# Two blocks' squares and scalings moved head by head to ScalarE, and one batch's last k and v loaded earlier

## The chip, the cores and the metric

The kernel runs on one NeuronCore of a Trainium2 chip. The metric is the device time of one execution in microseconds. The engines are TensorE (PE; PEld is its weight load), VectorE (DVE), ScalarE (ACT), GpSimd (POOL) and SyncE (SP, which here only issues transfers). Each takes its instructions in the order of its own queue and waits for semaphores of the others.

## What is computed

The reference chains three layers over 8 batches of 576 tokens, with 8 heads of 64 columns (4608 tokens, 512 columns):

```python
kv = np.einsum('bhsd,bhse->bhde', k, v)
out = np.einsum('bhsd,bhde->bhse', q, kv)
rms = np.sqrt(np.mean(out * out, axis=-1, keepdims=True) + 1e-06)
x = (out / rms * g_norm)                    # tokens x 512
h = x @ w_in                                # 512 x 2048
x = (np.maximum(h, 0) + alpha * np.minimum(h, 0)) @ w_out
logits = x @ w_gate; e = argmax(logits)     # one of 8 experts for each token
out[token] = gate_w * sigmoid(x @ w_output_gate)[e] * (relu(x @ w1[e]) @ w2[e])
```

The norm is one of each head: 64 columns are squared and summed for each token and head, and the head is multiplied by one number. This is where the change sits.

## The kernel before

Tokens are handled in 12 blocks of 384, three tiles of 128 tokens each. Products with weights are done in fp16 halves (a high and a low half for each f32 number), so x and every weight are split into halves first; the tiles of x are turned by a DMA before they serve as operand of the first dense layer.

The first two blocks are emitted by hand. The string `plan` is a list of words, and each word emits a few instructions; under `tc.manual_schedule` the queues of PE, DVE, ACT and SP keep exactly this order. Only POOL's order, and all that comes after the plan, is set by a scheduler. The plan mixes three things: the attention of blocks 0 and 1 (tiles 0 to 5), reading and splitting the 32 pieces of w_in and w_out, and the dense layers of blocks 0 and 1 as far as weights are ready.

The words for a tile t of attention: `q`/`Q` turn q by PE and copy it (ACT); `p` multiplies by kv into a PSUM bank (`ops`); `P` is `squares`: ACT writes the squares of the bank to `xs`; `s` is `sums`: DVE adds each head's 64 squares (`st`), scales them (`ms`), and POOL raises them to the power -1/2 (`rs`); `e` takes, once for each block, the exponents that put rows in fp16's range (DVE, small); `x` is `scaled`: DVE multiplies `rs` by the exponent and the bank by `rs`, head by head, into `xs`; `X`, `z`, `Z` make the high half (ACT), the low half (DVE) and issue the DMA that turns both (SP). A bank is free for other work of PE once `x` has read it. For block 0, `s`, `e` and `x` need all three tiles; tile 3 follows in the same queues.

The words for a weight piece i: `L` loads it (SP) into one of five raw buffers (`rawp`), `A` takes absolute values (ACT), `M` their maximum (DVE), `B` converts the bits (DVE, three instructions), `S` and `T` make the halves. A raw buffer is free after `B`, for the last four pieces of w_out after `T`. `H`, `C`, `R`, `G` are products, copy, leaky ReLU and halves of the first dense layer, `Y` the second.

k and v of a batch come as four pairs of heads; `n` is `load_kv`: two transfers (k, v) of a pair into a pool `kvp` with two buffers each, and with the first pair also the remainder of 64 rows (`kr`, `vr`). `k` is `kv_step`: PE multiplies a pair. In the plan pairs are loaded by `n` words. For batch 2 and later, which is handled after the plan, a step itself issues the load of the pair two further on, so pairs 2 and 3 of batch 2 are loaded once steps 0 and 1 are done. The first weights of the experts (`rawe`) use the five raw buffers next.

Of the kernel before, what the change touches and what calls it, by code (L numbers as in the profile page):

```python
# [10 lines left out]
F32 = mybir.dt.float32  # L11
F16 = mybir.dt.float16
BF16 = mybir.dt.bfloat16
I32 = mybir.dt.int32
AF = mybir.ActivationFunctionType
ALU = mybir.AluOpType
AX = mybir.AxisListType
# [3 lines left out]
P = 128  # L21
B, H, S, D = 8, 8, 576, 64
# [9 lines left out]
NPAIR = H // 2  # L32
TB = 3
# [3 lines left out]
QJ = 4  # L37
# [29 lines left out]
def body(ctx: ExitStack, tc, q, k, v, g_norm, w_in, w_out, alpha, w_gate, w_og, w1, w2, out):  # L67
    nc = tc.nc
    pe, dve, act, pool, sp = nc.tensor, nc.vector, nc.scalar, nc.gpsimd, nc.sync
# [36 lines left out]
    for G in range(B // 2):  # L106
        for half in range(2):
            b = 2 * G + half
# [52 lines left out]
    small = ctx.enter_context(tc.tile_pool(name="small", bufs=3))  # L161
# [27 lines left out]
    def right(name, bufs):  # L189
        return AR.enter_context(tc.tile_pool(name=name, bufs=bufs, side="right"))  # L190
# [4 lines left out]
    rawp, stg, cv = right("rawp", 5), right("stg", 2), right("cv", 2)  # L195
    kvp, qp, at = right("kvp", 2), right("qp", 2), right("at", 2)
# [16 lines left out]
    def load_kv(n):  # L213
        if n < len(kv_order):
            b, hp = kv_order[n]
            for nm, src in (("k", k), ("v", v)):
                if hp == 0:
                    t = kvp.tile([SR, H, D], F32, tag=nm + "r", name=f"{nm}r_{b}", bufs=1)
                    sp.dma_start(out=t, in_=src[b, :, QJ * P:S, :].rearrange("h p d -> p h d"))
                    kv_in[nm + "r", b] = t  # L220
                t = kvp.tile([P, 2, QJ, D], F32, tag=nm, name=f"{nm}_{b}_{hp}")
                sp.dma_start(out=t, in_=src[b, 2 * hp:2 * hp + 2, 0:QJ * P, :]
                             .rearrange("h (p j) d -> p h j d", j=QJ))
                kv_in[nm, n] = t
# [27 lines left out]
    def kv_step(n, pool_=None, tag="a"):  # L252
        b, hp = kv_order[n]
        kk, vv = kv_in.pop(("k", n)), kv_in.pop(("v", n))
        kr, vr = kv_in["kr", b], kv_in["vr", b]

        if hp % 2 == 0:
            kv_ps[b, hp // 2] = (pool_ or ps_a).tile([P, 2, D], F32, tag=tag, name=f"kvps_{b}_{hp}")
        ps = kv_ps[b, hp // 2]
        with tc.issue_after(paced["pe"]) if b > 2 else nullcontext():  # L260
            for j in range(QJ + 1):
                for i in range(2):
                    x, y = (kr[:, 2 * hp + i, :], vr[:, 2 * hp + i, :]) if j == 0 else (kk[:, i, j - 1, :], vv[:, i, j - 1, :])
                    pe.matmul(ps[64 * i:64 * i + 64, hp % 2, :], x, y, start=(j == 0), stop=(j == QJ))
        if b > 1:
            if hp % 2 == 1:
                kv_copy(n)
            load_kv(n + 2)

    def kv_copy(n):  # L270
        b, hp = kv_order[n]
        for i in range(2):
            sl = slice(64 * i, 64 * i + 64)
            (act.copy if b < 2 else dve.tensor_copy)(out=kvbd[b % 2][sl, hp - 1:hp + 1, sl], in_=kv_ps[b, hp // 2][sl])
# [19 lines left out]
    def att_parts(i):  # L294
        G, t0 = divmod(i * TB, 9)
# [3 lines left out]
        tiles = {}  # L299
# [59 lines left out]
        def squares(t):  # L359
            ops = tiles[t]  # L360
            xs = at.tile([P, DM], F32, tag="xs", name=f"xs_{G}_{t}", bufs=3)
            act.activation(out=xs, in_=ops.rearrange("p a b -> p (a b)"), func=AF.Square)
            tiles[t] = ops, xs

        def sums(t):
            nm = f"_{G}_{t}"
            ops, xs = tiles[t]
            if "st" not in tiles:
                tiles["st"] = small.tile([P, TB, H], F32, tag="st", name=f"st_{i}")
                tiles["qm"] = small.tile([P, TB], F32, tag="qm", name=f"qm_{i}")  # L370
            st = tiles["st"][:, t - t0, :]
            dve.tensor_reduce(out=st, in_=xs.rearrange("p (h d) -> p h d", h=H), axis=AX.X, op=ALU.add)
            if split_q:
                for _ in range(2):
                    dve.tensor_tensor(out=st, in0=st, in1=qi_[t], op=ALU.mult)
            ms = small.tile([P, H], F32, tag="ms", name="ms" + nm)
            dve.tensor_scalar(out=ms, in0=st, scalar1=1.0 / D, scalar2=EPS, op0=ALU.mult, op1=ALU.add)
            rs = small.tile([P, H], F32, tag="rs", name="rs" + nm)
            pool.tensor_tensor(out=rs, in0=ms, in1=mhalf, op=ALU.pow)  # L379
            tiles[t] = ops, xs, rs  # L380
# [15 lines left out]
        def scaled(t):  # L396
            ops, xs, rs = tiles[t]
            qm = tiles["qm"][:, t - t0:t - t0 + 1]
            if split_q:
                dve.scalar_tensor_tensor(out=rs, in0=rs, scalar=qm, in1=qi_[t], op0=ALU.mult, op1=ALU.mult)  # L400
            else:
                dve.tensor_scalar(out=rs, in0=rs, scalar1=qm, scalar2=None, op0=ALU.mult)
            dve.tensor_tensor(out=xs.rearrange("p (h d) -> p h d", h=H),  # L403
                              in0=ops.rearrange("p a (h d) -> p (a h) d", h=2),
                              in1=rs.unsqueeze(2).to_broadcast([P, H, D]), op=ALU.mult)

        def high(t):
            nm = f"_{G}_{t}"
# [12 lines left out]
        def x_turned(t):  # L421
            x16 = tiles.pop(t)[1]
            if i not in xt:
                xt[i] = xp.tile([P, 2 * NC, BLK], F16, tag="x", name=f"x_{i}")
            sp.dma_start_transpose(out=xt[i][:, :, (t - t0) * P:(t - t0 + 1) * P],
                                   in_=x16.rearrange("p a b -> p (a b)"))

        return ts, dict(q=turned, Q=turned_copy, t=tr, p=products, P=squares, s=sums, e=exponents, x=scaled, X=high, z=low,
                        Z=x_turned)

    def att_steps(i):
# [13 lines left out]
        if i == 2:  # L445
            for hp in range(NPAIR):
                kv_step(4 * nxt + hp)
                yield
            kv_halves(nxt)
            return  # L450
        kvs = [] if nxt is None or nxt >= B else [partial(kv_step, 4 * nxt + hp) for hp in range(NPAIR)]
        if kvs:
            kvs.append(partial(kv_halves, nxt))
# [947 lines left out]
    def emit(word):  # L1401
# [7 lines left out]
        elif what == "F":  # L1409
            y_scaled(*map(int, rest))  # L1410
        elif what in "UuVvW":
            scales(what, rest[0], int(rest[1]))
        elif rest[:1] in ("i", "o"):
            weights(what, dense[rest[0]], int(rest[1], 16))
        elif what == "k":
            n = int(rest)
            kv_step(n, *((ps_a, "a") if n < NPAIR else (ps_y, "y")))
        elif what == "c":
            scale_all()
        elif what in "fnNK":  # L1420
            dict(f=load_kv_first, n=load_kv, N=load_q, K=kv_copy)[what](int(rest))
        elif what == "D":
            i, u = map(int, rest)
            act.copy(out=accs[i][:, u, :], in_=ybank[i, u])
        elif what == "t":
            u = int(rest[1])
            src = accs[0][:, u, :]
            if rest[0] == "a":
                held["t", u] = row_scale(0, u, src, states[0][1])
            else:  # L1430
                (row_high, row_low)["bc".index(rest[0])](u, src, held["t", u])
        elif what == "q":
            t = int(rest)
            parts[t]["q"](t, *((ps_h, "h") if t < TB else (ps_y, "y") if t < 2 * TB else (ps_a, "a")))
        elif what == "e":
            parts[3 * int(rest)]["e"](3 * int(rest), 3 * int(rest) + 2)
        else:
            parts[int(rest)][what](int(rest))
# [15 lines left out]
    R021 Aie Lod Wo2 Loe H020 G021 n8 C022 Aif R022 H023 So9 Mie Soa n9 To9 F021 Bie F121 Y012 C023 G022 Sob  # L1454
    R023 Lof Aoc Mif F020 Y112 Bif F022 C020 So8 Tob G023 Aod H120 To8 F122 Ui3 Moc Mod ui3 H123 Bod C120 Vi3
    Y110 R020 Toa C123 Boc G020 vi3 F120 H121 R123 Aoe Wi3 Aof Moe G123 Y021 Sie Boe Sif Sid Sic Tie Y022 Tid
    Tif Tic R120 Mof H030 C121 Uo3 G120 Bof H130 C030 R121 R030 G121 G030 H032 C130 R130 uo3 G130 H033 Vo3 C032
    R032 G032 vo3 C033 H031 Wo3 Y121 c C031 Sof Sod Soc R031 Y020 F032 Tof G031 Toc F131 F031 Tod Soe R033 H132
    F030 Toe G033 H133 C132 R132 G132 Y031 C133 R133 G133 Y032 D01 ta1 Y030 D02 tb1 ta2 Y120 tc1 D00 tb2 ta0 q6
    tc2 F130 tb0 q7 Q6 tc0 q8 Q7 p6 H131 Q8 P6 s6 p7 C131 R131 p8 P7 G131 s7 Y122 P8 s8 e2 x6 Y130 F132 x7 X6 z6  # L1460
# [110 lines left out]
```

## Time and profile before

| | |
|---|---|
| median of three runs | 1340.95 us (1336.63 to 1350.32) |
| profiled execution | 1344.24 us |
| its span, first to last instruction | 1342.5 us |
| PE busy, share of the span | 1267.3 us, 94% |
| DVE busy | 824.4 us, 61% |
| ACT busy | 558.0 us, 42% |
| POOL busy | 413.7 us, 31% |
| mean granted clock of PE | 0.985 |

An engine is busy while an instruction of its own executes; waits and issues are not counted. The share is a mean over stages: in the page's 40 slices of 33.6 us, DVE is at nine tenths or more in the second to fourth and PE at five to eight in the first four; later PE is mostly at nine and DVE falls. The granted clock is TensorE's, as a share of full speed. A releaser (`<-`) is the instruction whose semaphore ended an engine's idle time.

### The profile page before, as it was taken

The numbers are of one execution on the slowest core, as the hardware profiler recorded it, in microseconds if no ns is written. First come the engines' busy times: TensorE is split into PE (matmuls) and PEld (weight loads), VectorE is DVE, ScalarE is ACT, GpSimd is POOL, SyncE is SP. The second block draws the span as 40 slices with busy tenths as digits, with TensorE's granted clock in tenths as the row PEclk, the third lists the DMA queues.
The fourth block names the chain that finished last, engine by engine and source line by source line (L and its number), as shares of the span: only waits on it lengthen the run. The fifth ranks groups of instructions, "written<-read, shape, count | busy, mean of one in ns | idle before, by whom it ended". The sixth has DMA issues, their size and how long they took to land. (4 is left out here: it accounts for less than half of the span.)

```text
span 1342.5 us, 22080 instructions
## 1 busy us (share of the span) xinstructions
PE 1267.3 (94%) x7681; PEld 661.5 (49%) x7681; DVE 824.4 (61%) x2254; ACT 558.0 (42%) x928; POOL 413.7 (31%) x490
## 2 busy tenths in 40 slices
PE   5688998999999989999999999999999999999998
PEld 4444455545454545545555555454434444444443
DVE  7999866989697877668687877463622221221221
ACT  4455553646564554555555665350111111111111
POOL 4322221544343442324242433222322222222211
PEclk9899998999999999999999999999999999999999
DMA  9563217695866756497745665209999799799842
GB/s 307 157 170 117 68 63 183 154 243 122 252 189 217 208 129 168 129 242 198 197 119 168 153 187 125 93 14 316 193 285 203 145 299 280 157 223 247 162 103 55
DMA packets 322497, 236.22 MB, mean 176 GB/s; under 512 B 245436, under 2 KB 278220, under 8 KB 317904
## 3 DMA queue, kind: packets, MB, share of 16 engines
q1 hardware_dynamic: 303760, 189.05, 56.3%
q0 software_dynamic: 9216, 28.94, 6.8%
q10 hardware_dynamic: 9408, 16.79, 3.7%
q8 instruction: 62, 1.02, 0.3%
q14 instruction: 51, 0.42, 0.1%
HBM read 252.54 MB, written 53.25 MB: 228 GB/s over the span
## 5 line engine op out<-in xcount | busy, mean ns | idle before, releaser
L766 PE MATMUL y<-wo,g 128*128 128x512 f16 x1728 | 394.2, 382 | 9.0 <-DVE xs L403 5.8
L726 PE MATMUL h<-x,wi 128*128 128x384 f16 x1920 | 336.8, 329 | 16.6 <-ACT m L732 15.8
L726 PEld LDWEIGHTS <-wi 128*128 128x128 f16 x2304 | 222.6, 99 | 176.5 <-issue 31.9
L766 PEld LDWEIGHTS <-g 128*128 128x128 f16 x1728 | 166.7, 98 | 202.2 <-issue 13.0
L749 POOL TENSOR_TENSOR g<-r,g 128x384 f16<-128x384 f32 x112 | 117.6, 1052 | 294.4 <-ACT g L748 235.8
L1276 DVE CAST h_d<-br_d 128x512 f16<-128x512 f32 x62 | 26.7, 430 | 257.2 <-DMA hT_d<-h_d 122.9
L742 DVE SCALAR_TENSOR_TENSOR r<-m,alphat 128x384 f32<-128x384 f32 x192 | 133.2, 696 | 31.0 <-ACT m L732 27.5
L748 ACT CAST g<-r 128x384 f16<-128x384 f32 x192 | 97.2, 509 | 116.6 <-DVE r L742 116.1
L1292 PEld LDWEIGHTS <-hT_d 128*128 128x128 f16 x744 | 72.8, 98 | 93.1 <-DMA hT_d<-h_d 4.1
L1270 PEld LDWEIGHTS <-byT_d 128*128 128x128 f16 x744 | 72.6, 98 | 88.2 <-issue 0.8
L732 ACT ACTIVATE m<-h,scal 128x384 f32<-128x384 f32 x160 | 92.1, 577 | 53.0 <-PE h L726 51.2
L379 POOL TENSOR_TENSOR rs<-ms,mhalf 128x8 f32<-128x8 f32 x36 | 66.2, 1839 | 135.1 <-DVE qm L385 87.0
L479 DVE SCALAR_TENSOR_TENSOR wlo_w<-rawe,es_w,whi_w 128x1024 f16<-128x1024 f32 x64 | 84.4, 1324 | 28.0 <-ACT whi_w L478 13.3
L1296 POOL DMA_INDIRECT out_dram<-ob_d,oidx_d x31 | 32.5, 1050 | 195.6 <-ACT ob_d L1295 185.2
L1274 ACT ACTIVATE br_d<-bh_d 128x512 f32<-128x512 f32 x62 | 37.0, 597 | 127.4 <-PE bh_d L1270 113.0
L1292 PE MATMUL bo_d<-lane,hT_d 128*128 128x512 f16 x360 | 81.7, 384 | 3.0 <-DMA hT_d<-h_d 3.0
L478 ACT ACTIVATE whi_w<-rawe,es_w 128x1024 f16<-128x1024 f32 x64 | 72.2, 1142 | 29.3 <-DMA ws<-whi_w 14.2
L1270 PE MATMUL bh_d<-lane,byT_d 128*128 128x512 f16 x360 | 80.2, 379 | 0.0
L1295 ACT ACTIVATE ob_d<-bo_d,msc_d 128x512 f32<-128x512 f32 x31 | 21.3, 687 | 141.0 <-PE bo_d L1292 141.0
L628 ACT ACTIVATE eab_w<-rawe 128x1024 bf16<-128x1024 f32 x64 | 66.6, 1051 | 25.6 <-DMA rawe<-in_moe_w_dram 21.8
L726 PE MATMUL hbank<-x,wi 128*128 128x384 f16 x384 | 67.0, 332 | 6.7 <-DMA x<-x 4.9
L913 POOL DMA_INDIRECT ytab<-row,pos x36 | 42.1, 1168 | 73.4 <-DMA ytab<-row,pos 42.6
(386 smaller groups left out, 1594.2 us busy)
## 6 DMA issues: line engine op xcount, KB each, us to landing
lane<-ws SPq DMA_DIRECT2D x74, 1024.0 KB
wi<-ws SPq DMA_DIRECT2D x44, 1024.0 KB
wo<-ws SPq DMA_DIRECT2D x36, 1024.0 KB
rawe<-in_moe_w_dram SPq DMA_DIRECT2D x64, 512.0 KB
ws<-whi_w ACTq DMA_DIRECT2D x64, 256.0 KB
ws<-wlo_w SPq DMA_DIRECT2D x64, 256.0 KB
rawwi<-in_moe_w_in_dram SPq DMA_DIRECT2D x16, 512.0 KB
rawwo<-in_moe_w_out_dram SPq DMA_DIRECT2D x16, 512.0 KB
```

Source lines behind the costliest of these rows:

```text
L379: pool.tensor_tensor(out=rs, in0=ms, in1=mhalf, op=ALU.pow)
L478: act.activation(out=dst_h, in_=src, func=AF.Copy, scale=s)
L479: dve.scalar_tensor_tensor(out=dst_l, in0=src, scalar=s, in1=dst_h, op0=ALU.mult, op1=ALU.subtract)
L628: act.activation(out=ab.rearrange("p a b -> p (a b)"), in_=raws[4 * m + i], func=AF.Abs)
L726: t = pe.matmul(ps, wi[:, f // 4 * NC + c, w, fs], xt[i][:, xc, :], start=(n == 0), stop=(n == 3 * NC - 1))
L732: t = act.activation(out=r0, in_=ps, func=AF.Copy, scale=(scst if start else scal)[:, f:f + 1])
L742: t = dve.scalar_tensor_tensor(out=r, in0=r0, scalar=alphat[:, f:f + 1], in1=r0, op0=ALU.mult, op1=ALU.max)
L748: act.copy(out=hi, in_=r)
L749: (pool if start or f % 2 else dve).tensor_tensor(out=lo, in0=r, in1=hi, op=ALU.subtract)
L766: t = pe.matmul(ps, g[:, t, f % GF, us], wo[:, f, w, :], start=(start and m == 0), stop=(stop and m == 2), **kw)
L1270: pe.matmul(hp[ts], j["yT"][:, x, ts], w1_[:, w, c, hs], start=(m == 0), stop=(m == 3 * NC - 1))
L1292: pe.matmul(po[ts], hT[:, g, ts], w2_[:, w, f, :], start=(m == 0), stop=(m == 3 * NFE - 1))
```

## The change

Three things are edited. In blocks 0 and 1 (`i < 2`), `squares` becomes eight activations of 64 columns, each with an accumulator output that gives the head's sum, so that DVE's sum goes; and `scaled` becomes eight ACT copies of 64 columns, each with the head's `rs` as scale, in place of DVE's multiplication. Block 2 and later keep the old form. Pairs 2 and 3 of batch 2 (n = 10 and 11) are loaded by two new words of the plan, `n10 n11`, behind the bits of w_out's last piece, into raw buffers instead of `kvp`. And the steps of batch 2 no longer load two pairs further on; its last step loads the first two pairs of batch 3.

```diff
@@ load_kv
-                t = kvp.tile([P, 2, QJ, D], F32, tag=nm, name=f"{nm}_{b}_{hp}")
+                if n in (4 * 2 + 2, 4 * 2 + 3):
+                    if nm == "k":
+                        both = rawp.tile([P, 512, 2], I32, tag="raw", name=f"kv_{b}_{hp}")
+                        both = both.rearrange("p a b -> p (a b)").bitcast(F32).rearrange(
+                            "p (x h j d) -> p x h j d", x=2, h=2, j=QJ)
+                    t = both[:, "kv".index(nm)]
+                else:
+                    t = kvp.tile([P, 2, QJ, D], F32, tag=nm, name=f"{nm}_{b}_{hp}")
@@ kv_step
-            load_kv(n + 2)
+            for m in ((n + 2,) if b > 2 else (n + 1, n + 2) if hp == NPAIR - 1 else ()):
+                load_kv(m)
@@ squares
-            act.activation(out=xs, in_=ops.rearrange("p a b -> p (a b)"), func=AF.Square)
+            if i < 2:
+                src = ops.rearrange("p a (h d) -> p (a h) d", h=2)
+                for h in range(H):
+                    act.activation(out=xs[:, h * D:(h + 1) * D], in_=src[:, h, :], func=AF.Square,
+                                   accum_out=tiles["st"][:, t - t0, h:h + 1])
+            else:
+                act.activation(out=xs, in_=ops.rearrange("p a b -> p (a b)"), func=AF.Square)
@@ sums
-            dve.tensor_reduce(out=st, in_=xs.rearrange("p (h d) -> p h d", h=H), axis=AX.X, op=ALU.add)
+            if i >= 2:
+                dve.tensor_reduce(out=st, in_=xs.rearrange("p (h d) -> p h d", h=H), axis=AX.X, op=ALU.add)
@@ scaled
-            dve.tensor_tensor(out=xs.rearrange("p (h d) -> p h d", h=H),
-                              in0=ops.rearrange("p a (h d) -> p (a h) d", h=2),
-                              in1=rs.unsqueeze(2).to_broadcast([P, H, D]), op=ALU.mult)
+            src = ops.rearrange("p a (h d) -> p (a h) d", h=2)
+            if i < 2:
+                for h in range(H):
+                    act.activation(out=xs[:, h * D:(h + 1) * D], in_=src[:, h, :], func=AF.Copy, scale=rs[:, h:h + 1])
+            else:
+                dve.tensor_tensor(out=xs.rearrange("p (h d) -> p h d", h=H), in0=src,
+                                  in1=rs.unsqueeze(2).to_broadcast([P, H, D]), op=ALU.mult)
@@ plan
-    Tif Tic R120 Mof H030 C121 Uo3 G120 Bof H130 C030 R121 R030 G121 G030 H032 C130 R130 uo3 G130 H033 Vo3 C032
+    Tif Tic R120 Mof H030 C121 Uo3 G120 Bof n10 n11 H130 C030 R121 R030 G121 G030 H032 C130 R130 uo3 G130 H033 Vo3 C032
```

The queue of ACT in block 0, from the third tile's squares to the fourth's (the last number of a name's first three is the tile; `kvbd` belongs to k and v, `uwo` to the weights). Before:

```order
L362 ACTIVATE xs_0_2_509<-ops_0_2_480 128x512
L517 ACTIVATE uwo3_531<-rawwo3_420 128x512
L274 COPY kvbd1_206<-kvps_1_0_495 64x2x64 x2
L414 CAST x16_0_0_556<-xs_0_0_447 128x512
L414 CAST x16_0_1_560<-xs_0_1_478 128x512
L414 CAST x16_0_2_563<-xs_0_2_509 128x512
L362 ACTIVATE xs_0_3_566<-ops_0_3_551 128x512
```

Now:

```order
L376 ACTIVATE xs_0_2_521,st_0_448<-ops_0_2_493 128x64 x8
L536 ACTIVATE uwo3_549<-rawwo3_420 128x512
L282 COPY kvbd1_206<-kvps_1_0_507 64x2x64 x2
L421 ACTIVATE xs_0_0_447<-ops_0_0_424,rs_0_0_471 128x64 x8
L421 ACTIVATE xs_0_1_484<-ops_0_1_458,rs_0_1_505 128x64 x8
L433 CAST x16_0_0_588<-xs_0_0_447 128x512
L421 ACTIVATE xs_0_2_521<-ops_0_2_493,rs_0_2_547 128x64 x8
L433 CAST x16_0_1_599<-xs_0_1_484 128x512
L433 CAST x16_0_2_602<-xs_0_2_521 128x512
L376 ACTIVATE xs_0_3_605,st_1_606<-ops_0_3_583 128x64 x8
```

Three rows became forty, and the scalings, which stood in DVE's queue, now stand between the third tile's squares and the fourth's.

The queue of SP after the plan's last weight load (`yT` are turned rows of block 0's result, `k_3_0` is pair 0 of batch 3). Before:

```order
L616 DMA rawe_0_2287<-in_moe2_w1_dram 128x1024
L616 DMA rawe_1_2289<-in_moe2_w1_dram 128x1024
L616 DMA rawe_2_2291<-in_moe2_w1_dram 128x1024
L616 DMA rawe_3_2293<-in_moe2_w1_dram 128x1024
L616 DMA rawe_4_2295<-in_moe2_w2_dram 128x2x512
L425 DMA_TRANSPOSE x_2_2109<-x16_0_6_2090 128x8x128
L425 DMA_TRANSPOSE x_2_2109<-x16_0_7_2093 128x8x128
L425 DMA_TRANSPOSE x_2_2109<-x16_0_8_2113 128x8x128
L833 DMA_TRANSPOSE yT_0_0_2141<-row0_193 128x8x128
L833 DMA_TRANSPOSE yT_0_1_2143<-row1_194 128x8x128
L232 DMA q_1_0_2147<-in_q_dram 128x8x128
L232 DMA q_1_2_2149<-in_q_dram 128x8x128
```

Four transfers of k and v of pairs 2 and 3 (`k_2_2`, `v_2_2`, `k_2_3`, `v_2_3`) came next. Now, from the new loads on, and then what stands behind q:

```order
L229 DMA kv_2_2_1774<-in_k_dram 128x2x256
L229 DMA kv_2_2_1774<-in_v_dram 128x2x256
L229 DMA kv_2_3_1777<-in_k_dram 128x2x256
L229 DMA kv_2_3_1777<-in_v_dram 128x2x256
L635 DMA rawe_0_2363<-in_moe2_w1_dram 128x1024
L635 DMA rawe_1_2365<-in_moe2_w1_dram 128x1024
L635 DMA rawe_2_2367<-in_moe2_w1_dram 128x1024
```

```order
L239 DMA q_1_2_2231<-in_q_dram 128x8x128
L229 DMA k_3_0_2283<-in_k_dram 128x2x256
L219 DMA kr_3_2281<-in_k_dram 64x8x64
L219 DMA vr_3_2285<-in_v_dram 64x8x64
L229 DMA v_3_0_2287<-in_v_dram 128x2x256
L229 DMA k_3_1_2289<-in_k_dram 128x2x256
L229 DMA v_3_1_2291<-in_v_dram 128x2x256
L635 DMA rawe_3_2369<-in_moe2_w1_dram 128x1024
L635 DMA rawe_4_2371<-in_moe2_w2_dram 128x2x512
```

The loads of batch 2's last pairs moved ahead of the expert weights, batch 3's first loads took their place behind q, and two expert loads moved behind those.

PE's queue after the plan (steps of k and v of batch 2, then h of block 2). Before, where pairs 2 and 3 followed only after 43 matmuls of h:

```order
L264 MATMUL kvps_2_0_2151<-v_2_1_1483,k_2_1_1481 64x64 x8
L264 MATMUL kvps_2_2_2182<-vr_2_1456,kr_2_1452 64x64 x2
L726 LDWEIGHTS wi_203
L726 MATMUL h_2_0_2237<-x_2_2109,wi_203 128x384
```

Now:

```order
L271 MATMUL kvps_2_0_2235<-v_2_1_1561,k_2_1_1559 64x64 x8
L271 MATMUL kvps_2_2_2258<-vr_2_1534,kr_2_1530 64x64 x2
L271 MATMUL kvps_2_2_2258<-kv_2_2_1774 64x64 x8
L271 MATMUL kvps_2_2_2258<-vr_2_1534,kr_2_1530 64x64 x2
L271 MATMUL kvps_2_2_2258<-kv_2_3_1777 64x64 x8
L745 LDWEIGHTS wi_203
L745 MATMUL h_2_0_2313<-x_2_2193,wi_203 128x384
```

All four steps now stand together, and batch 3's first step follows 36 matmuls of h and eight of the gate's logits later.

## Rows read from the trace of the kernel before

**Rows 1.** Stretches: length; PE, PEld, DVE, ACT, POOL busy; PE clock, DMA share, GB/s.

```profile
27.50:31.77 4.27, 4.27 (x52) 3.69 (x52) 4.17 (x8) 3.85 (x8) 2.55 (x2) 1.00 1.04 403
50.00:80.00 30.00, 21.81 (x95) 10.45 (x96) 28.61 (x72) 13.29 (x23) 7.73 (x6) 0.83 0.44 116
80.00:135.00 55.00, 49.83 (x280) 26.79 (x279) 52.56 (x117) 31.51 (x59) 16.61 (x14) 1.00 0.45 139
135.00:200.00 65.00, 63.17 (x379) 34.18 (x378) 49.15 (x120) 37.22 (x68) 18.81 (x17) 1.00 0.21 66
214.00:225.00 11.00, 8.54 (x70) 4.92 (x68) 5.27 (x12) 2.43 (x4) 0.73 (x1) 0.69 0.93 250
```

**Rows 2.** Waits of DVE from 11 to 80 us: total, times, longest.

```profile
DVE wi L559 <- ACT wi L557: 0.5, 1, 0.5
DVE r L742 <- ACT m L732: 0.3, 1, 0.3
```

**Rows 3.** PE in order of time: start, duration, instructions [idle before, releaser].

```profile
50.27 7.04 PE L726 MATMUL hbank<-x,wi 128*128 128x384 f16 x32 [2.83 <-DMA x<-x]
...
65.76 7.94 PE L766 MATMUL y<-wo,g 128*128 128x512 f16 x24 [5.85 <-DVE xs L403]
...
78.78 11.86 PE L726 MATMUL hbank<-x,wi 128*128 128x384 f16 x72 [2.07 <-DMA x<-x]
```

**Rows 4.** DVE in order of time, blocks 0 and 1.

```profile
32.51 0.08 DVE L524 DVE_READ_ACCUMULATOR uwo<-uwo 128x1 f32 x1
32.51 0.68 DVE L372 TENSOR_REDUCE st<-xs 128x8 f32<-128x512 f32 x1
33.23 0.18 DVE L377 TENSOR_SCALAR ms<-st 128x8 f32<-128x8 f32 x1
...
34.77 0.69 DVE L403 TENSOR_TENSOR xs<-ops,rs 128x512 f32<-128x512 f32 x1
...
39.76 0.17 DVE L377 TENSOR_SCALAR ms<-st 128x8 f32<-128x8 f32 x1
...
64.92 0.69 DVE L403 TENSOR_TENSOR xs<-ops,rs 128x512 f32<-128x512 f32 x1
...
68.22 0.69 DVE L419 TENSOR_TENSOR x<-xs,x 128x512 f16<-128x512 f32 x1
```

**Rows 5.** ACT's groups by form: shapes, count, busy us, mean ns, idle before.

```profile
L362 ACT ACTIVATE xs<-ops 128x512 f32<-128x512 f32 x36 | 21.3, 591 | 10.3 <-PE ops L353 9.8 <-PE ops L356 0.5
...
L274 ACT COPY kvbd<-kvps 64x128 f32<-64x128 f32 x8 | 2.0, 255 | 0.7 <-PE kvps L264 0.6
...
L478 ACT ACTIVATE wg<-wgr,swg 128x16 f16<-128x16 f32 x4 | 0.9, 300 | 0.0
```

**Rows 6.** ACT in order of time: squares of tiles 0, 2 and 3.

```profile
27.50 0.60 ACT L362 ACTIVATE xs<-ops 128x512 f32<-128x512 f32 x1 [0.18 <-PE ops L356]
...
31.77 0.58 ACT L362 ACTIVATE xs<-ops 128x512 f32<-128x512 f32 x1
...
38.06 0.60 ACT L362 ACTIVATE xs<-ops 128x512 f32<-128x512 f32 x1
```

**Rows 7.** PE in order of time, after the plan.

```profile
207.81 6.01 PE L726 MATMUL h<-x,wi 128*128 128x384 f16 x36 [0.54 <-DMA x<-x]
...
216.99 0.69 PE L264 MATMUL kvps<-v,k 128*64 128x64 f32 x16 [1.82 <-DMA v<-in_v_dram]
...
218.57 1.12 PE L264 MATMUL kvps<-v,k 128*64 128x64 f32 x16 [0.64 <-DMA v<-in_v_dram]
...
221.47 3.67 PE L726 MATMUL h<-x,wi 128*128 128x384 f16 x12
```

**Rows 8.** SP's queue in order of time: issue, duration, transfers.

```profile
171.43 3.55 SPq L616 DMA_DIRECT2D rawe<-in_moe_w_dram  x4
...
210.33 1.50 SPq L222 DMA_DIRECT2D k<-in_k_dram  x1
211.88 0.46 SPq L222 DMA_DIRECT2D v<-in_v_dram  x1
```

More of the change, by code (lines that the diff above doesn't have):

```diff
@@ L361, in squares @@
             xs = at.tile([P, DM], F32, tag="xs", name=f"xs_{G}_{t}", bufs=3)
-            act.activation(out=xs, in_=ops.rearrange("p a b -> p (a b)"), func=AF.Square)
+            if "st" not in tiles:
+                tiles["st"] = small.tile([P, TB, H], F32, tag="st", name=f"st_{i}")
+                tiles["qm"] = small.tile([P, TB], F32, tag="qm", name=f"qm_{i}")
+            if i < 2:
[5 more added lines that the diff above has]
+                act.activation(out=xs, in_=ops.rearrange("p a b -> p (a b)"), func=AF.Square)
             tiles[t] = ops, xs
@@ L367, in sums @@
             ops, xs = tiles[t]
-            if "st" not in tiles:
-                tiles["st"] = small.tile([P, TB, H], F32, tag="st", name=f"st_{i}")
-                tiles["qm"] = small.tile([P, TB], F32, tag="qm", name=f"qm_{i}")
             st = tiles["st"][:, t - t0, :]
-            dve.tensor_reduce(out=st, in_=xs.rearrange("p (h d) -> p h d", h=H), axis=AX.X, op=ALU.add)
+            if i >= 2:
+                dve.tensor_reduce(out=st, in_=xs.rearrange("p (h d) -> p h d", h=H), axis=AX.X, op=ALU.add)
             if split_q:
```

## The prediction, made before the change was run

> **What bounds the kernel now.** I began with the run's totals: the profiled execution took 1344.24 us, its span is 1342.5 us, and TensorE (PE) is busy in 94% of it. The chain of waits of the page does not help here: it begins only after 1121 us, and everything that is edited runs before about 220 us. So I cut that part into stretches [rows 1]. From 135 to 200 us PE is busy in 63.17 of 65 us: there it is the bound, and nothing that it is late by can be made up. From 50 to 135 us VectorE (DVE) is busy in 81.2 of 85 us, PE in 71.6: there DVE sets the pace. The waits of DVE confirm it: between 11 and 80 us it has waited 0.8 us for others, all told [rows 2]. PE's own rows in this part show what it waits for [rows 3]: for the x tiles of block 0 at 50.27 us, for a PSUM bank that DVE's scaling frees at 65.76 us (5.85 us), and for the x tiles of block 1 at 78.78 us. All three end the same path: squares, sums, exponents, scaling, fp16 halves, a turning DMA. A change of that path's length moves PE by as much, and since the later stretches are full, it stays to the end.
>
> **The change on DVE.** Six sums over 128x512 and six scalings of 128x512 go. A sum lasts 0.68 us and a scaling 0.69; the next instruction starts 0.72 after a sum, of which some 0.1 is a wait for its result [rows 4], so one holds the queue for about 0.60. That is 12 x 0.6 = 7.3 us less work on the engine that sets the pace. It would be the gain, if DVE never had to wait for what replaces it.
>
> **The change on ScalarE (ACT).** Each of six tiles gets 8 squares of 128x64 with an accumulator output, and 8 copies of 128x64 with a scale read from a column, in place of one square of 128x512 and of DVE's scaling. Neither form is in the trace, so I bound both. From PSUM, 512 columns take 591 ns and 128 take 255 [rows 5]: 0.875 ns a column, so 64 columns take 255 - 56 = 199 ns. Neighbours can overlap: the four 128x16 with a column scale take 300 ns each and 0.9 us in all, so they start 0.20 us apart, 0.10 less than they last [rows 5]. The accumulator has to be read out; DVE's own reading shows as a row of 0.08 us, and the next instruction starts at the same time as it [rows 4].
> - A head's square: at least 0.10 us (overlapped, the reading free), at most 0.40 (no overlap, and the reading as dear as a whole small instruction, 0.20). I take 0.30 = 199 ns + 0.1 for the reading, without overlap, because a reading must follow the end of what it reads. A tile's squares: S = 2.4 us (0.8 to 3.2).
> - A head's scaled copy: 0.20 us apart at 16 columns, and 48 columns more by 0.875 ns: 0.24 us; at most 0.34, without overlap. A tile: C = 1.9 us (1.6 to 2.7).
>
> **Block 0, along ACT's queue.** ACT's order is written out, so nothing overtakes. The first square starts at 27.50 and the third at 31.77 [rows 6]. Between them ACT was busy for 3.85 us [rows 1], two squares of some 0.55 and 2.75 us of other work. Now: 27.50 + 3 x 2.4 + 2.75 = 37.45 for the end of the third tile's squares. From the sum's follower on DVE (33.23) to the first scaling (34.77) it is 1.54 us [rows 4], unchanged, since the exponents stay on DVE: the first scaling starts at 39.1, 4.3 us later than before. Then three scalings and three casts stand in ACT's queue ahead of the fourth tile's squares: 3 x 1.9 + 3 x 0.52 = 7.3 us (a cast taken as the 591 ns of 512 columns less some overlap), so those start at 46.4 instead of 38.06 [rows 6], and end at 48.8. DVE takes that tile's statistics before the bits of w_out's pieces 2 and 3. It did so at 39.76 [rows 4], and now does at 48.8: **9.05 us late**, with some 13 us of DVE idle in which its saving of four sums and three scalings disappears. What is queued behind it: those bits free the raw buffer that SP's next load of w_out waits for, and behind that load stands the last turning DMA of block 0. So PE's start at 50.27 moves by the same 9 us, and DVE's weights too.
>
> **Block 1.** Here two more sums leave a DVE that has no gap: 9.05 - 1.2 = 7.85. The first scaling goes from 64.92 [rows 4] to 72.8, PE's bank is free at 74.7 instead of 65.6, three scalings end at 78.5 (3 x 1.9), and one cast later the first low half starts on DVE at 79.0, where it was 68.22 [rows 4]. That is **+10.7 us** at the x tiles for which PE waits at 78.78 [rows 3]. From there to 200 us DVE and PE have the same work as before and both are that much later, so the 10.7 us stay.
>
> By the Trainium skill, ScalarE: Activation LUTs, section What ACT_TABLE_LOAD costs, an ACTIVATE takes 186 ns plus 0.833 ns a column, a pointer operand adds 93 ns, and neighbours overlap by 93 ns. That would make a head's square 0.146 us without its reading, which the page does not price, and a copy 0.239; by the same steps the delay would be 6.0 us, and the time 1343.5. For 128 columns it gives 293 ns where the row shows 255 [rows 5]. The same page's Rules for kernel authors put multiplications on VectorE, not ScalarE; in this trace one f32 tile of 128x512 from PSUM is no dearer on ACT (0.59) than on DVE (0.69) [rows 5, 4], so what speaks against the change here is eight starts in place of one, not the engine.
>
> **The early transfers.** Before, PE stopped at 216.99 (1.82 us) and 218.57 (0.64) for batch 2's k and v, whose loads were issued only at 210.33 and behind [rows 7, 8], and the stretch 214 to 225 ran at a granted clock of 0.69 [rows 1]: 12 matmuls took 3.67 us in it, where 36 take 6.01 elsewhere [rows 7]. Idle and clock together cost 5.1 us there; 0.54 us of waiting for x at 207.81 would be covered too. Those four transfers now stand where the first expert weights were issued, at 171.43 [rows 8], 35 us before they are used, in a stretch with a DMA share of 0.21 [rows 1]: they are there in time. But the same place of SP's queue is now taken by batch 3's loads, six of them, behind the same two turning DMAs. The first v landed 216.99 - 211.88 = 5.1 us after its issue [rows 8, 7]; the remainder of batch 3's v is third in the line, so it lands near 217. PE now reaches it after the two k-v steps that it no longer skips (1.4 us from 207.27, where it began to wait for x), 36 matmuls of h (6.01) and eight small ones (0.2): 214.9 [rows 7]. About 2 us of the wait stay, with a part of the clock. Gain 3.5 us, between 1 (the wait only changes its name) and 6 (it goes whole). Two expert loads now come after batch 3's. They are the last two of five and are used in turn, so the first three cover them, and I cost that at nothing; if they were late, ACT's absolute values of expert weights would be, which PE needs only at the end of the kernel.
>
> **Sum.** 10.7 - 3.5 = +7.2 us against the profiled 1344.24: 1351.4. The median of the runs is 1340.95, 3.3 below the profiled one, so I predict **1348 us**.
>
> **Rivals.**
> 1. ACT's pieces are cheap (S = 0.8, C = 1.6). Same steps: statistics 1.8 us late, first low half of block 1 2.65 late; with a transition gain of 5 us that is 1338.6. For it: ACT is idle for half of the part, and 0.20 us apart is measured. Against: a reading per head. 20%.
> 2. ACT's pieces are dear (S = 3.2, C = 2.7), and the wait at the third tile's squares decides: statistics 14.7 late, block 1's low half 18.9 late, the transition gives 2: 1357.8, slower by over 1%. The point is about 0.36 us per head for squares with 0.28 for copies. Against: it needs no overlap anywhere. 17%.
> 3. DVE's relief reaches the end: ACT is never waited for, 7.3 + 5.6 us are won: 1328. For it: DVE has no gap. Against: the third scaling and the fourth square are one after another in one queue. 5%.
> 4. The transfers are not early: the second waits in SP's queue until w_out's piece 12 is split and its buffer free. The expert loads of before waited for the same buffers and were out by 175 us [rows 8], so I give it 3%; it would be 1351.
>
> My forecast has 55%: between +2 and +13 us.
>
> **Numbers.** 1% (13.4 us) is about what a measurement here can tell from no change. The range takes the forecast, the cheap case and most of the dear one: 1337 to 1361. Faster by over 1%: 6% (rival 3 and a little). Slower: 22% (rival 2 and the upper end of the forecast). Within: 72%.
>
> **What would show it.** In the profile after: the squares of a head 0.25 to 0.35 us apart and a row of their own for the reading; DVE idle of some 10 us before 50 us, put down to ACT's squares, casts or scalings; PE's start on h near 59 instead of 50.27, and on block 1 near 89 instead of 78.78; at about 215 to 220 (plus the delay) one shorter wait of PE for v of batch 3, and none for batch 2. I am wrong if DVE keeps under 2 us of idle in 11 to 80 us, or if the late start at 50 us is made up before 200 us.

## The result, and the profile after

The changed kernel took 1353.67 us (median of 20 runs, 1347.44 to 1362.29), the kernel before, run beside it, 1346.20 (20 runs). The ratio is 1.0068, with a 95% interval of 1.0050 to 1.0087: 9.2 us slower (6.7 to 11.7). That is within 1%, as forecast; the predicted difference was +7.2 us. The profiled execution took 1357.35 us with a span of 1355.6. Single executions of one kernel lie up to 17 us apart, so times are compared by medians of many runs, and a profile is read for places.

In the stretches of [rows 1], after the change:

```profile
27.50:31.77 4.27, 4.27 (x48) 3.62 (x48) 2.24 (x4) 3.52 (x23) 1.46 (x1) 1.00 1.05 401
50.00:80.00 30.00, 20.59 (x95) 10.85 (x96) 22.92 (x57) 20.24 (x78) 7.69 (x6) 0.83 0.42 107
80.00:135.00 55.00, 47.44 (x253) 24.84 (x252) 51.97 (x120) 29.83 (x54) 14.47 (x12) 0.97 0.49 145
```

DVE, which was full from 50 to 80 us (28.61 of 30), is busy in 22.92, ACT in 20.24 in place of 13.29, and PE has gained nothing from it: 20.59 against 21.81. What DVE does instead of work stands in its waits from 11 to 95 us, where the kernel before waited for ACT 1.2 us in all ([rows 2], which end at 80 us, have 0.8):

```profile
DVE x L438 <- ACT x L433: 8.5, 3, 3.8
DVE ms L392 <- ACT xs L376: 5.4, 4, 1.9
DVE r L761 <- ACT m L751: 3.8, 3, 1.5
```

The first is the low half, which waits for ACT's cast behind the scalings; the second is the statistics, which wait for ACT's squares. The third is the copy of h, for which ACT itself waits for PE. DVE in order of time, beside [rows 4]:

```profile
36.08 0.17 DVE L392 TENSOR_SCALAR ms<-st 128x8 f32<-128x8 f32 x1 [0.94 <-ACT xs L376]
...
41.52 0.69 DVE L438 TENSOR_TENSOR x<-xs,x 128x512 f16<-128x512 f32 x1 [3.29 <-ACT x L433]
...
45.83 0.17 DVE L392 TENSOR_SCALAR ms<-st 128x8 f32<-128x8 f32 x1 [0.87 <-ACT xs L376]
...
76.37 0.69 DVE L438 TENSOR_TENSOR x<-xs,x 128x512 f16<-128x512 f32 x1 [3.76 <-ACT x L433]
```

The fourth tile's statistics come at 45.83 instead of 39.76 (+6.1), block 1's first low half at 76.37 instead of 68.22 (+8.15). PE follows, beside [rows 3]:

```profile
56.59 10.71 PE L745 MATMUL hbank<-x,wi 128*128 128x384 f16 x48 [3.08 <-DMA x<-x]
...
72.61 1.01 PE L785 MATMUL y<-wo,g 128*128 128x512 f16 x2 [5.32 <-ACT xs L421]
...
86.51 13.32 PE L745 MATMUL hbank<-x,wi 128*128 128x384 f16 x72 [3.25 <-DMA x<-x]
```

All three starts are later, by 6.3, 6.85 and 7.7 us, and the second now waits for ACT's scaling, no longer for DVE's. The 72 matmuls at 86.51 take 13.32 us where they took 11.86: a part of them runs at the lower of the clock's two levels (1.2 and 2.4 GHz), and the mean granted clock of 80 to 135 us is 0.97 in place of 1.00.

The prices of the new pieces, ACT in order of time (columns as in [rows 6]):

```profile
28.27 0.22 ACT L376 ACTIVATE xs<-ops 128x64 f32<-128x64 f32 x1 [0.75 <-PE ops L364]
28.39 0.19 ACT L376 ACTIVATION_READ_ACCUMULATOR xs<-ops 128x1 f32 x1
28.49 0.21 ACT L376 ACTIVATE xs<-ops 128x64 f32<-128x64 f32 x1
...
29.86 0.77 ACT L576 ACTIVATE wi<-wo,scol 128x512 f16<-128x512 f32 x1
...
37.60 3.38 ACT L421 ACTIVATE xs<-ops,rs 128x64 f32<-128x64 f32 x16 [0.70 <-DVE rs L417]
40.75 0.73 ACT L433 CAST x<-xs 128x512 f16<-128x512 f32 x1
```

Each head's square has a row of its own for reading the sum, which the listing of ACT's queue does not show: two rows of squares there became forty of squares and scalings (not three rows, as said below the listing), and sixteen readings come on top. Eight heads hold the queue from 28.27 to 29.86: S = 1.59 us a tile, 0.20 a head. Sixteen scaled copies go from 37.60 to 40.75: C = 1.58 a tile, also 0.20 a head. Both prices are read off the starts: the same group by form (48 instructions, 10.3 us, mean 323 ns) would give 0.32 and count overlapped time twice.

```profile
L376 ACT ACTIVATE xs<-ops 128x64 f32<-128x64 f32 x48 | 10.3, 323 | 0.8 <-PE ops L364 0.8
L421 ACT ACTIVATE xs<-ops,rs 128x64 f32<-128x64 f32 x48 | 10.3, 394 | 1.4 <-DVE rs L417 1.4
```

The transition, PE in order of time, beside [rows 7], and SP's queue, beside [rows 8]:

```profile
216.55 0.69 PE L271 MATMUL kvps<-kv 128*64 128x64 f32 x16
...
218.04 4.07 PE L745 MATMUL h<-x,wi 128*128 128x384 f16 x24
...
227.37 0.33 PE L271 MATMUL kvps<-vr,kr 64*64 64x64 f32 x4 [3.00 <-DMA vr<-in_v_dram]
...
235.52 4.77 PE L745 MATMUL h<-x,wi 128*128 128x384 f16 x28
...
268.85 0.40 PE L866 MATMUL l<-wg,yT 128*128 128x32 f16 x8 [4.39 <-DMA yT<-row]
```

```profile
180.78 0.37 SPq L229 DMA_DIRECT2D kv<-in_k_dram  x1
181.20 0.46 SPq L229 DMA_DIRECT2D kv<-in_v_dram  x1
...
221.95 0.62 SPq L219 DMA_DIRECT2D vr<-in_v_dram  x1
```

And before, in the same part, behind the rows of [rows 7]:

```profile
229.65 4.06 PE L726 MATMUL h<-x,wi 128*128 128x384 f16 x24
...
235.09 2.11 PE L726 MATMUL h<-x,wi 128*128 128x384 f16 x12 [1.38 <-ACT m L732]
...
237.95 4.06 PE L726 MATMUL h<-x,wi 128*128 128x384 f16 x24 [0.62 <-ACT m L732]
...
243.12 0.84 PE L353 MATMUL ops<-kv,qT 128*128 128x128 f16 x12 [1.11 <-DMA qT<-q]
```

Batch 2's four k-v steps run without a stop. One wait of 3.00 us for batch 3's vr remains, as long as the three of before together (0.54, 1.82 and 0.64 us). Before the steps PE is 9.3 us late (214.53 against 205.19). At 235.52 it is 5.9 us later than before's 229.65, but it has then done 60 matmuls of h where before had done 72, with the same six k-v steps; the twelve take 2.0 us, so at equal work 1.5 us are won by then. More comes behind it, since before's waits at 235.09, 237.95 and 243.12 us are not there: when 132 matmuls of h and all eight k-v steps of batches 2 and 3 are done, the change is 4.7 us late (251.1 against 246.4), so 4.6 us are won. Forty microseconds after the wait for vr stands one of 4.39 us for the turned rows yT, which the kernel before did not have.

### The profile page after: what moved, and what is told of

Same layout as the page of the kernel before. It is cut to its first block, busy times and chain, and to the rows that moved or that the text cites. A ratio compares the mean times of both kernels' runs of the same rounds, so it can differ in the third digit from the quotient of the medians.

```text
span 1355.6 us, 22196 instructions
## 1 busy us (share of the span) xinstructions
PE 1271.3 (94%) x7681; PEld 662.3 (49%) x7681; DVE 818.3 (60%) x2242; ACT 573.5 (42%) x1066; POOL 417.3 (31%) x490
## 5 line engine op out<-in xcount | busy, mean ns | idle before, releaser
L785 PEld LDWEIGHTS <-g 128*128 128x128 f16 x1728 | 166.6, 98 | 199.5 <-issue 10.1
L1314 ACT ACTIVATE ob_d<-bo_d,msc_d 128x512 f32<-128x512 f32 x31 | 21.3, 687 | 140.1 <-PE bo_d L1311 140.1
```

The lines of the kernel that those rows point to most:

```text
L785: t = pe.matmul(ps, g[:, t, f % GF, us], wo[:, f, w, :], start=(start and m == 0), stop=(stop and m == 2), **kw)
```

## The experiments

What they gave, each against the kernel before, run beside it. "h 0" and "h 1" are PE's starts on h of blocks 0 and 1 and "k-v" its first k-v step after the plan, in the profiled execution; the clock is the mean granted clock of all runs of that kernel (10 to 12; 20 for the change, 4 for the half heads, 29 or 17 for before). The squares without sums, the last but one below, ran once, and only its profile is used.

| kernel | ratio (95%) | h 0 | h 1 | k-v | clock |
|---|---|---|---|---|---|
| before | 1 | 50.27 | 78.78 | 205.19 | 0.988 |
| the change | 1.0068 (1.0050 to 1.0087) | 56.59 | 86.51 | 214.53 | 0.980 |
| transfers alone | 1.0003 (0.9978 to 1.0029) | 50.21 | 78.39 | 204.77 | 0.983 |
| transfers, q's loads later | 1.0003 (0.9967 to 1.0040) | 51.00 | 79.07 | 205.44 | 0.985 |
| ScalarE's part alone | 1.0077 (1.0054 to 1.0101) | 56.16 | 83.70 | 210.26 | 0.984 |
| squares alone | 1.0019 (0.9989 to 1.0050) | 53.46 | 82.05 | 209.68 | 0.988 |
| scalings alone | 1.0047 (1.0019 to 1.0075) | 54.48 | 84.91 | 211.23 | 0.984 |
| change, words moved | 1.0027 (1.0007 to 1.0046) | 54.10 | 82.15 | 210.41 | 0.984 |
| change, half heads | 1.0110 (1.0075 to 1.0144) | 59.38 | 91.88 | 220.87 | 0.977 |
| transfers, block 1's squares | 1.0016 (0.9983 to 1.0050) | 51.14 | 77.87 | 204.26 | 0.984 |

**Which part costs.** ScalarE's part alone: batch 2's loads put back.

```diff
-            for m in ((n + 2,) if b > 2 else (n + 1, n + 2) if hp == NPAIR - 1 else ()):
-                load_kv(m)
+            load_kv(n + 2)
-                if n in (4 * 2 + 2, 4 * 2 + 3):
+                if n < 0:
-    ... Bof n10 n11 H130 ...
+    ... Bof H130 ...
```

> The squares and scaled copies of the change, batch 2's k and v loaded as in the kernel before. Theory (ScalarE's longer chain is all of the loss): tile 3's statistics near 45.8, h near 56.6, block 1's h near 86.5 as with the whole change, the four k-v steps 9 us later than before, and the time 9 to 13 us above before, ratio 1.007 to 1.010. Rival (the delay is taken up by the transition's wait, since the waited-for transfers of batch 2 do not move with PE): the delay shrinks by 3 to 5 us at 215 to 230, ratio 1.003 to 1.005. Rival B (the loss is of the transfers): ratio 1.000.

It is 10.3 us slower than before (7.3 to 13.6), as much as the whole change. In time the theory holds and both rivals fall: the transition does not take the delay up. Its places were met for block 0's h alone (56.16): block 1's h is 4.9 us late, not 7.7, and the k-v steps 5.1, not 9, although ACT's queue is the same as in the change. The 48 matmuls of block 0 took 7.96 us there and 10.71 in the change's profile: where a stretch at the lower clock falls differs from run to run, and it moves a single profile by 2 to 4 us. That execution was also 6.5 us faster than the median of its kernel.

The transfers alone: the conditions `i < 2` of squares and scalings set to `i < 0`, and the sums to `i >= 0`.

> Squares and scaled copies as in the kernel before, the early transfers of batch 2's k and v kept. Theory (the two parts are separate, the transfers give about 3.4 us in the transition and nothing else): the first statistics of tile 3 near 39.8 and PE's start on h near 50.3 again, as before; batch 3's vr is waited for near 218 for about 3 us in place of batch 2's k and v; 3 to 4 us faster than before, ratio near 0.9975. Rival A (the transfers are hidden or cost as much elsewhere, the transition's shift is given back behind 235): ratio 1.000. Rival B (the transfers are part of the loss): slower than before by 3 us or more.

The expected 3 to 4 us are not there: +0.4 us (-3.0 to +3.9). Blocks 0 and 1 stand as before, and the four steps at 204.77 run through, as expected. But PE's rows show what follows:

```profile
217.66 0.48 PE L271 MATMUL kvps<-vr,kr 64*64 64x64 f32 x4 [3.06 <-DMA vr<-in_v_dram]
...
260.43 0.40 PE L866 MATMUL l<-wg,yT 128*128 128x32 f16 x8 [4.90 <-DMA yT<-row]
```

The second wait is the one of the change at 268.85. It is in the profiles of all six kernels that have the early transfers (3.4 to 4.9 us) and in none of the five without them: there PE has y matmuls to do in front of the same l, and waits for 3.5 us at most, for an exponent on DVE, ahead of these. With batch 2's steps earlier the order of PE behind them comes out otherwise, with l ahead of that work. The stretches around it, of before and then of the transfers alone (columns as in [rows 1]):

```profile
256.00:263.00 7.00, 5.98 (x31) 2.82 (x30) 7.00 (x33) 4.12 (x7) 1.58 (x2) 1.00 0.48 93
263.00:270.00 7.00, 7.00 (x50) 3.67 (x49) 6.96 (x10) 5.52 (x8) 5.53 (x4) 1.00 1.09 254
```

```profile
256.00:263.00 7.00, 2.57 (x16) 1.39 (x17) 7.00 (x17) 5.72 (x9) 5.97 (x6) 0.67 0.93 219
263.00:270.00 7.00, 7.00 (x37) 3.03 (x36) 7.00 (x13) 4.65 (x6) 2.69 (x3) 0.84 1.02 332
```

PE loses 3.4 us of busy time there (5.98 to 2.57), and in the next 7 us, busy all the time, it works at a granted clock of 0.84 where before had 1.00. Part of this is made up behind it, where before has waits of its own. From the first of the four steps to batch 4's first one, a stretch of some 135 us, the six profiles with the transfers take 132.7 to 137.1 us, mean 134.8, and the five without them 134.5 to 136.6, mean 135.6. In the transfers' own profile next to nothing is won at the transition itself (the same 72 matmuls of h and six steps take 24.3 us, before 24.5; over all profiles 21.3 to 25.6 with the transfers and 21.7 to 24.5 without), and 3.3 us by the point of 132 matmuls; at batch 4 the mean gain is 0.8, less than the profiles scatter.

The other wait, taken up by itself: q's loads 5 and 6 moved behind the drain of the attention steps.

```diff
-    for n in (5, 6):
-        load_q(n)
     attq.append(att_steps(2))
     behind.close()
     drain(attq)
+    for n in (5, 6):
+        load_q(n)
```

> The early transfers alone (squares and scaled copies as before), and the two loads of q 5 and 6 issued after the attention steps, so that batch 3's k and v stand 1.2 us earlier in SyncE's queue. Theory (PE's wait near 218 is for the landing of batch 3's vr, and what is won there holds): the wait of 3.1 us with the transfers alone shrinks to about 1.9, and the time is 3 to 5 us below before, ratio 0.996 to 0.998. Rival (what the transfers win by 235 us is given back behind it, at the turned rows of yT near 260): the wait shrinks, the ratio stays at 0.999 to 1.002. Rival B (the moved loads of q come too late for their own users): slower than before by 1 us or more.

```profile
216.45 0.33 PE L271 MATMUL kvps<-vr,kr 64*64 64x64 f32 x4 [1.37 <-DMA vr<-in_v_dram]
...
259.17 0.39 PE L866 MATMUL l<-wg,yT 128*128 128x32 f16 x8 [3.55 <-DMA yT<-row]
```

The wait for vr shrank to 1.37 us, so it is the landing behind SP's queue (vr landed 1.2 us earlier, and PE came 0.5 us later); the time did not move (+0.4 us, -4.4 to +5.4), which is the rival's figure, though the interval does not exclude the theory's. The yT wait stayed.

**Squares or scalings.** Each alone, with batch 2's loads as before.

> Of the change only the squares and their sums head by head on ScalarE; the scaled copies on VectorE and batch 2's k and v as in the kernel before. Theory (the squares' 1.58 us a tile lengthen the chain, but without the scalings ScalarE's queue has room again before the fourth tile): first scaling about 2.8 us later than the 34.8 of before, PE's h of block 0 2 to 4 us later than 50.3, block 1's h 2 to 4 us later than 78.8, ratio to before 1.002 to 1.003. Rival A (the squares are nearly all of the loss): ratio 1.006 or more. Rival B (VectorE, rid of 0.6 us of sum a tile, gains more than ScalarE's queue loses): block 0's h earlier than 50.3, ratio 1.000 or below.

> Of the change only the scaled copies head by head on ScalarE; squares, sums and batch 2's k and v as in the kernel before. Theory (three copies of 1.58 us stand before the first cast and the fourth tile's squares, VectorE waits for each, and block 1 has the same again): first scaling at its old 34.8, PE's h of block 0 2 to 4 us later, block 1's h 5 to 7 us later than 78.8, ratio to before 1.004 to 1.006, so that squares and scalings make up the 10 us of both. Rival A (the copies are hidden, VectorE is what was full): ratio 1.000 to 1.001. Rival B (the two do not add, each alone costs nearly all): ratio 1.007 or more.

Squares alone: block 0's h 3.2 us later, block 1's 3.3, time +2.5 us (-1.5 to +6.7). Scalings alone: 4.2 and 6.1 us later, time +6.3 (2.6 to 10.1). Both theories hold in the main (block 0's 4.2 us is just above the 2 to 4 expected): by the medians the two sum to 8.8 us against 10.3 together, and two thirds is the scalings', which stand in the path of both blocks. With intervals of some 4 us either way that split is rough, and the squares' loss alone is not clear of nothing in time.

**Is it the queue's order?** Two pieces of the written order moved, so that DVE has work where it stood.

```diff
-    ... X0 x2 X1 z0 X2 z1 P3
-    z2 Z1 s3 k6 Bo2 k7 Mo3 Ai4 Li7 Z2 Bo3 K7 ...
+    ... X0 x2 X1 Bo2 Mo3 Bo3 z0 X2 z1 P3
+    z2 Z1 s3 k6 k7 Ai4 Li7 Z2 K7 ...
-    ... X3 X4 Mi7 Y001 X5 z3 Bi7 Z3 Y002 Ui1 z4
+    ... X3 X4 Mi7 Bi7 Ui1 Y001 X5 z3 Z3 Y002 z4
```

> The whole change, and two pieces of the written-out order moved: Bo2, Mo3 and Bo3 (4.2 us of VectorE's work) ahead of the first low half of block 0, Bi7 (1.8 us) and Ui1 ahead of block 1's first partial sum, so that VectorE does them while it would stand and wait for ScalarE. Theory (the loss is VectorE's waiting behind ScalarE's in-order queue, 14 us of it between 11 and 95 us, and work that fits into it comes off behind it): PE's h of block 1 starts 3 to 6 us earlier than with the change, and the time is 3 to 6 us below that of the change, about 1.003 of before. Rival (the path runs on ScalarE's own queue, VectorE's waits are only its shadow): block 1's h within 1 us of the change's 86.5, ratio to before 1.007. Rival B (the moved work holds up the low halves): 2 to 4 us slower than the change.

```profile
DVE r L761 <- ACT m L751: 5.4, 3, 2.7
DVE ms L392 <- ACT xs L376: 4.9, 4, 1.9
DVE x L438 <- ACT x L433: 2.3, 2, 1.7
```

The low halves' wait went from 8.5 us to 2.3, that for the copy of h rose from 3.8 to 5.4, and the three together fell from 17.7 to 12.6. Block 1's h starts 4.4 us earlier than with the change, which is hardly more than a single profile moves by itself; but the time is 5.5 us below it (ratio 1.0027 against 1.0068, intervals that do not touch), and 6.7 below ScalarE's part alone, run beside it. The theory holds, and the rival that DVE's waits are only a shadow falls. What remains is slower than before still.

**The dose, and the price of a piece.** The scaled copies in two pieces of 32 columns:

```diff
-                for h in range(H):
-                    act.activation(out=xs[:, h * D:(h + 1) * D], in_=src[:, h, :], ...
+                for h in range(2 * H):
+                    hs = slice(h % 2 * D // 2, (h % 2 + 1) * D // 2)
+                    act.activation(out=xs[:, h * D // 2:(h + 1) * D // 2], in_=src[:, h // 2, hs], ...
```

> The whole change with each scaled copy in two pieces of 32 columns: 16 starts a tile in place of 8. Theory (a small copy on ScalarE costs its start, 0.197 us apart whatever its columns, so the scaled copy of a tile goes from 1.58 to 3 us or a little more, and three of them stand in the path of block 0, six in that of block 1): tile 3's statistics 4 to 5 us later than with the change, block 1's h 8 to 9 us later, the time 7 to 10 us above the change, ratio to before near 1.013. Rival (cost goes by columns, halves start 0.13 us apart or less): 0 to 3 us above the change, ratio 1.007 to 1.009. Rival B (ScalarE's chain is not in the path): no difference, ratio 1.007.

```profile
42.48 3.22 ACT L422 ACTIVATE xs<-ops,rs 128x32 f32<-128x32 f32 x16
45.21 1.52 ACT L435 CAST x<-xs 128x512 f16<-128x512 f32 x2
```

Sixteen starts take 2.73 us (42.48 to 45.21), 0.17 each: half the columns save only 0.03, so by these two widths 0.14 of a start is there whatever its width. C grew by 1.15 us, not by 1.4 or more; Tile 3's statistics (48.41) are 2.6 us later than with the change, h is 2.8 us later in block 0 and 5.4 in block 1, and the time is 5.6 us longer (four runs, so give or take some 5). By the theory's own count (three copies in block 0's path, six in block 1's) that price gives 3.4 and 6.9. Size missed, direction and count nearly met. The rival by columns falls by the price, since it asked for at most 0.13 us a start; its time, at most 3 us, the few runs do not exclude.

The squares without their sums, DVE adding up as before:

```diff
-                    act.activation(..., func=AF.Square, accum_out=tiles["st"][:, t - t0, h:h + 1])
+                    act.activation(..., func=AF.Square)
```

> Squares head by head on ScalarE without their sums (the sums on VectorE, scaled copies and transfers as in the kernel before): eight squares of 64 columns a tile and no read of the accumulator. It prices the read row. Theory (the read is an instruction of its own in ScalarE's queue and half of a head's 0.195 us): one head's square starts 0.10 to 0.14 us after the last, 0.8 to 1.1 us a tile. Rival (the read is hidden behind the next start, a start costs what a scaled copy's does): 0.17 to 0.20 us, 1.4 to 1.6 us a tile.

```profile
27.26 1.01 ACT L375 ACTIVATE xs<-ops 128x64 f32<-128x64 f32 x8
28.08 0.79 ACT L574 ACTIVATE wi<-wo,scol 128x512 f16<-128x512 f32 x1
```

Eight squares take 0.82 us, 0.10 each. So the reading is the other half of a head's 0.20, as the theory had it.

**A version that beats both?** Squares with sums on ScalarE in block 1 alone, where ACT has room, and the early transfers.

> The early transfers, and the squares with their sums on ScalarE in block 1 alone; all else as in the kernel before. Squares in both blocks put h 3.2 us later in block 0 and 3.3 us later in block 1, so nearly all of their loss came from block 0. Theory (block 0's squares stand on the path to its scalings, block 1's stand where ScalarE is idle for half of the time, and VectorE is rid of 1.8 us there): block 0's h near 50.3 as before, block 1's h 1 to 2 us earlier than 78.8, PE's wait for block 1's scaled tile shorter than the 5.8 us of before, ratio to before 0.997 to 1.000. Rival (the squares cost ScalarE's queue as much in block 1): block 1's h 2 to 4 us later, ratio 1.001 to 1.003.

```profile
65.15 7.03 PE L785 MATMUL y<-wo,g 128*128 128x512 f16 x24 [4.37 <-DVE xs L423]
...
77.87 11.86 PE L745 MATMUL hbank<-x,wi 128*128 128x384 f16 x72 [2.69 <-DMA x<-x]
```

In its profile the theory nearly holds: block 0's h is 0.9 us late, block 1's 0.9 early (1 to 2 expected), the wait for the scaled tile 4.37 us in place of 5.85. In time the ratio of 1.0016 (0.9983 to 1.0050) is the rival's figure, though its interval holds the theory's too; a gain is not shown. None of these versions was measured faster than the kernel before.

## Why the prediction came out right, by its steps

- **The place and the mechanism** were right. DVE's saved work did not arrive, because ACT's queue runs in order and DVE waits behind it: 10.2 us of idle before 50 us (some 13 expected), put down to squares and casts as said. Moving words into these gaps brought 5.5 us back. The starts of h came earlier than its signs (59 and 89 us; 56.59 and 86.51 measured), for the reason that follows.
- **S and C were mis-sized.** S = 2.4 and C = 1.9 us were taken; 1.59 and 1.58 were measured. For S the error is in "without overlap": by its row the reading does not wait for the end of what it reads, since it starts 0.12 us after the first square, which lasts 0.22. For C it is the 0.24 us a head, where 0.20 was measured. By the prediction's own steps the measured prices give 4.8 us for the fourth tile's statistics (9.05 forecast, 6.1 measured) and 5.5 us for block 1's first low half (10.7 forecast, 8.15 measured). Of what is above 4.8, 0.8 is PE's own later start in that execution (28.27 against 27.50).
- **"The 10.7 us stay."** That a delay stays was right: it is 7.7 us at block 1's h and 9.3 at the k-v steps in the profile of the change, 4.9 and 5.1 in that of ScalarE's part alone. That 10.7 lies near the +10.3 measured for that part is in part luck. With the measured prices the same steps give 5.5 us, which lies between the two profiles' 4.9 and 7.7; the other 5 us or so of the medians come from something that the sum lacked, and no profile shows it at a place. The granted clock is a candidate: its mean over the runs is 0.980 for the change, 0.984 for ScalarE's part and 0.988 for before. With levels of 1.2 and 2.4 GHz 0.980 is 54 us of a span at the lower one, 0.988 is 32 (an estimate). What that costs was not tried by itself. In two sets of 29 runs of before, an execution with a clock lower by 0.001 was longer by 0.9 and 1.7 us (least squares), which need not be its cause; the transfers alone ran at 0.983, with a time only 0.4 us above before's. Nor do longer waits always bring more of the lower level: h of block 0 took 9.64 us before, 10.71 with the change, but 7.96 with ScalarE's part alone. So this term stays open.
- **The transition's 3.5 us.** The exchange came as told: batch 3's vr is waited for in place of batch 2's k and v. The step that was mis-sized is "about 2 us of the wait stay": 3.00 us stayed with the change and 3.06 with the transfers alone, as much as went, so the wait only changed its name, the lower end of the prediction's range. (PE was there at 214.60 in the transfers' profile, 214.9 forecast; vr landed at 217.66, forecast near 217.) At equal work the place itself gave 1.5 and 0.2 us; the 4.6 and 3.3 us won a little later come from three waits of before that the prediction did not count. And they do not reach the end: the transfers alone changed the time by +0.4 us (-3.0 to +3.9), which just leaves out a gain of 3.5. The profiles show one place where it goes, the yT wait and the slower stretch behind it. The other candidate is the clock of these runs, 0.983: 0.0046 below before, by the slopes above 4 to 8 us (an estimate). How the loss divides between the two stays open.
- So +10.7 and -3.5 were forecast, and +10.3 and about 0 measured (each within 3 us or a little more): the sum of +7.2 lies in the measured 6.7 to 11.7. It is the sum that was met: ScalarE's term was priced too high for what it held, the transition's gain did not come, and a loss that it did not hold made up for both. Rival 3 (1328) is excluded by the time. Rival 1 had the price of the copies right (1.6) and the squares' too low (0.8, which is what squares without the reading take); rival 2's prices were not seen. Rival 4 is excluded by the issue of the second pair at 180.78, 35 us before its use at 216.55.
- Against the absolute 1348: the three runs shown of before had a median of 1340.95, the 20 beside the change 1346.20. That shift of 5 us, not the change, is most of what the figure misses.

## What to carry to other kernels

Work moved from a full engine to a half-idle one pays only if the idle engine's queue is not on the path at that place: count what stands in its order between the inputs and the waiter, by the price of a start and not only by columns. A full engine's relief appears as its own waiting unless other work is ordered into the gap. And a wait removed in front of a scheduled stage should be followed through the next ones, at equal work done, before it is counted: here a wait of the same length took its place, and another stood 40 us later, with a lower clock behind it.

## What the runs showed of the hardware that was not expected

- A square of 64 columns from PSUM starts 0.10 us after the last; with an accumulator output there is a second instruction, and a head takes 0.20. A copy with its scale from a column takes 0.20 without any reading. Recorded durations in such a chain grow (0.22 to 0.41 us in the first three tiles) while the starts stay 0.20 apart, so only starts give the price.
- DVE's row for yT, 0.74 us as a rule, lasted 3.77 to 3.98 us in four of the six kernels with early transfers. With the transfers alone:

```profile
252.16 3.64 DVE L132 TENSOR_SCALAR pw_eq<-qam 128x8 int32<-128x8 int32 x1
...
252.35 3.98 DVE L843 SCALAR_TENSOR_TENSOR row<-g,sr,row 128x512 f16<-128x512 f32 x1
...
257.18 0.74 DVE L843 SCALAR_TENSOR_TENSOR row<-g,sr,row 128x512 f16<-128x512 f32 x1
```

```profile
252.75 1.16 POOL L438 TENSOR_TENSOR x<-xs,x 128x512 f16<-128x512 f32 x1
253.87 0.91 POOL L768 TENSOR_TENSOR g<-r,g 128x384 f16<-128x384 f32 x1
254.74 1.04 POOL L296 TENSOR_TENSOR kvsc<-kvbd,kvs 128x512 f32<-128x512 f32 x1
```

  The long row ends at 256.33, after three POOL instructions in a row that end at 255.78, and the turning of yT is issued at 256.36. By the Trainium skill, SBUF — State Buffer, section SBUF: two separate sides, a DVE instruction with two SBUF inputs and a GpSimd one that reads SBUF take a shared port pair in turn, and the loser blocks for the whole of the other's instruction. The trace agrees as far as its times go: both inputs are in SBUF, and the row ends behind POOL's, three of them in place of one. But three small rows just in front of it, the first at 252.16, carry 3.5 to 3.6 us too, so which of these four was held, and that a port held it, is not shown. The long row makes up only a part of the yT wait: this is 4.4 to 4.9 us in the four kernels with the long row and 3.4 and 3.6 in the two without.
